# One stay of TensorE in its 64x64 tiles for each unit of a linear-attention and GELU-FFN kernel, with k transposed there by fp32 products

## The chip, the cores and the metric

The kernel runs on one core of a Trainium2 chip. The metric is the device time of one execution in microseconds (us): from the start of the program on the core to its end. Lower is better. Five engines are named by the profile: PE (TensorE, matrix products), with PEld for its weight loads, DVE (VectorE), ACT (ScalarE), POOL (GpSimd) and SP (SyncE, which issues most transfers here).

## The reference

Two stages follow each other. A gated linear attention keeps, for each of 4 batches and 8 heads, a 48x48 state that decays row by row with alpha and takes in the outer product of k and v at each of 768 positions; y is q times the state. The 3072 rows of y (8 heads x 48 = 384 columns) then go through a feed-forward net with 2048 hidden columns and an exact GELU.

```python
for t in range(S):                       # S = 768, D = 48
    state = alpha[:, :, t, :, None] * state + np.einsum('bhd,bhe->bhde', k[:, :, t], v[:, :, t])
    y[:, :, t] = np.einsum('bhd,bhde->bhe', q[:, :, t], state)
x = y.transpose(0, 2, 1, 3).reshape(B * S, H * D)     # 3072 x 384
h = x @ w_in                                          # 384 x 2048
g = 0.5 * h * (1.0 + erf(h / sqrt(2)))
out = g @ w_out                                       # 2048 x 384
```

## The kernel before

**Attention by units.** Positions are taken 256 at a time (12 groups, `g`), the heads in two halves (`u`), so there are 24 units, n = 2g + u. Names carry both numbers: `yc_3_0` belongs to g = 3, u = 0, which is unit 6. On DVE a unit's decays are run up as products (two scans forward, `pp`, two backward, `rp`), q is multiplied by the first and k by the second. On PE a unit has four steps, each of many small fp32 products that fill one of four 64x64 tiles of the array:

- `scores` (S, L351): k by q in four chunks of 64 positions, 16 products with 64 columns each. The profile shows an fp32 product as two rows, so 32 rows.
- `turned` (T, L359): k transposed, since the state needs it with positions along the partitions. Four 128x128 transposes against the identity, on the whole array.
- `inside` (I, L410 and L427): the masked scores by v, 16 products (32 rows), which begin y; then the turned k by v, 16 products with 48 columns (32 rows, 24 for the last group of a batch), which give the growth of the state by chunks.
- `outside_part` (O, L477): the states by q, which completes y: 16 products with 64 columns (32 rows), 12 (24 rows) for the first group of a batch.

Between S and I, DVE writes the masked scores (`ss`, L387) and ACT the turned k (`kn`, L381) to SBUF. Between I and O, DVE adds up the chunks' states (`chain`, L447). After O, y is split into a rounded float32r part and a remainder (`xh` on ACT, `xl` on DVE; for units 0 to 2 the remainder is made by a product with minus the identity on PE, `x_minus`, L562, and an ACT copy).

**Where a unit's results stand.** For the units 2 to 11, S and T of unit n write the same PSUM bank pair (`sbank` or `ybank`) in which I and O of unit n - 2 and of unit n itself build y. From unit 12 (`SPLIT`) on, S writes two other banks (`sh`, `sw`) and every y is built in `sbank`. So either S of unit n, or I of unit n - 1, can't start before y of unit n - 2 has been read. For units 4 to 9 that reading is one ACT copy of y to SBUF (`yc`, L557, `y_out`), and the split works from the copy; for the others the split itself reads the bank.

**The net.** Four blocks of 256 rows (`gemm1` L585, `gemm2` L677) and four of 512 rows (`wide1` L602, `wide2` L620) are multiplied in steps of 256 or 128 hidden columns. Each step is a first product, two GELU activations on ACT (`ghi` L654, rounded; `hp` or `hw` L658, in full), their difference on DVE (`glo`, L667) and a second product. x, the weights and the GELU's result are each split in two float32r parts, of which three products are taken. The weights are turned into such parts in 16 pieces during the first 85 us (ACT `top` L265 and L279, DVE L269 and L282, for pieces 1 to 3 with help of PE, L291).

**What sets the order.** A planner at build time places all steps on PE, DVE, ACT and SP by a table of costs (`COST`), by ranks (`ORDER`: digits are units, letters weight pieces) and by dependencies (`op(...)` in `plan_unit`). The order on each engine is then fixed; the hardware waits only for data. PE takes attention steps when they are ready, and steps of the net otherwise. `JOINED`, `SEAM`: from unit 6 on, the planner ties O, I and S of neighbouring units so that some of them follow each other directly.

Of the kernel before, what the change touches and what calls it, by code (L numbers as in the profile page):

```python
# [8 lines left out]
F32 = mybir.dt.float32  # L9
# [13 lines left out]
BY_PRODUCT = (1, 2, 3)  # L23
EARLY = 2
JOINED = 5
SEAM = 0.22
U_RANK, HI_RANK = 0.5, 0.4
X_BY_PRODUCT = (1, 2)
STEPS_BY_PRODUCT = 2
LOOK, EARLY_LOOK = 1.5, 1.0  # L30
RATE = 360.0
# [1 line left out]
WAIT = 0.2  # L33
SLOW = 1.0
COST = dict(
    turn=0.3, head=0.75, body=0.95, tail=0.49, sel=0.6, sel2=1.0, ends=0.22, differ=1.2, half=0.34, minus=0.4, gminus=0.35, rest=0.5, rest2=1.0,
    scan=0.65, scan2=0.65, back0=0.86, back=0.71, times=0.62, q=1.35, scores=1.24, kn=0.52, mask=0.62, mask1=0.4, kn1=0.36, inside=1.28, chain=1.1, outer=0.77, carry=0.22,
    xh=0.6, xl=0.72, spread=2.0, check=0.85, load=2.6, fetch=0.4, u=1.0, c0=0.56, c1=0.89, c2=0.56, c3=0.95, c4=0.92,
    hi=0.82, lo=0.89, gemm1=2.12, gelu=0.51, low=0.62, most=1.4, last=0.69, part=1.0,
    wide1=2.1, wide2=2.07, wpart=1.1,  # L40
)
ORDER = "0 1 a b c 2 d 3 e f 4 g h i j k 5 l m n o p"


@with_exitstack
def gla_then_gelu_ffn(ctx: ExitStack, tc: tile.TileContext, q, k, v, alpha, qg, kg, ag, vg, w_in, w_out, out):
    nc = tc.nc
    B, H, D, S = q.shape
    NF, P, NK, _ = w_in.shape
    DM, DFF = NK * P, NF * P  # L50
    NT = B * S
    C = 128
    G = 2 * C
    CS = C // 2
# [300 lines left out]
    def turned(g, u):  # L355
        d = cur[g, u]
        for j in range(NCH):
            e = (2 + j % 2) * C
            nc.tensor.transpose(  # L359
                out=d["s"][j // 2][:, e : e + C], in_=d["kt"][:, 2 * j * CS : 2 * (j + 1) * CS], identity=ident  # L360
            )

    def room(n):
        return stage if n % 2 and n < NU * NSB else work

    def kn_tile(g, u):
        d = cur[g, u]
        if "kn" not in d:
            d["kn"] = room(NU * g + u).tile([P, 2, 2 * P], F32, tag="kn", bufs=1, name=f"kn_{g}_{u}")
        return d["kn"]  # L370

    def ss_tile(g, u):
# [5 lines left out]
    def turned_out(g, u, bank=None):  # L378
        src = y_of(NU * g + u) if bank is None else cur[g, u]["s"][bank]
        to = kn_tile(g, u)  # L380
        nc.scalar.copy(to if bank is None else to[:, bank], src[..., 2 * C : 4 * C])  # L381

    def masked(g, u, bank=None):
        src = y_of(NU * g + u) if bank is None else cur[g, u]["s"][bank].unsqueeze(1)
# [9 lines left out]
    def inside(g, u):  # L394
        d = cur[g, u]
        ybank = y_of(NU * g + u)
        vn = vbuf[g % NB]
        spare = () if g else (0, 1)[: u + 1]
        for i in spare:
            nc.tensor.matmul(  # L400
                ybank[:, i, :G], lhsT=zeros, rhs=products[:, :G], start=True, stop=False, skip_group_check=True
            )
        for j in range(NCH):
            for i in range(2):
                r = slice(i * CS, (i + 1) * CS)
                for h in range(2):
                    rows = D if i in spare else DP
                    o = slice((h ^ i) * DP, (h ^ i) * DP + rows)
                    e = (2 * u + h) * D
                    nc.tensor.matmul(  # L410
                        ybank[o, i, j * CS : (j + 1) * CS],
                        lhsT=vn[r, j, e : e + rows],
                        rhs=d["ss"][r, h, j, :],
                        start=(j == 0 and i not in spare),
                        stop=(j == 0 and g % GPB == 0),
                        skip_group_check=True,
                    )
        for j in range(NCH):
            if ends_batch(g, j):
                continue  # L420
            t = 2 * C + j * D
            for i in range(2):
                r = slice(i * CS, (i + 1) * CS)
                for h in range(2):
                    o = slice(h * DP, (h + 1) * DP)
                    e = (2 * u + h) * D
                    nc.tensor.matmul(  # L427
                        ybank[o, i, t : t + D],
                        lhsT=d["kn"][r, j // 2, (j % 2) * P + h * DP : (j % 2) * P + (h + 1) * DP],
                        rhs=vn[r, j, e : e + D],  # L430
                        start=False,
                        stop=True,
                        skip_group_check=True,
                    )
# [400 lines left out]
    def op(*args, **kw):  # L835
        ops.append(Op(*args, **kw))
        return ops[-1]
# [4 lines left out]
    def plan_unit(n):  # L842
# [25 lines left out]
        d["back"] = op("DVE", "back", lambda: fns["b"](1), [half], rank=r)  # L868
        d["keys"] = op("DVE", "times", lambda: fns["k"](), [d["back"]], rank=r)
        shared = [pp_.get("out", pp_["xh"]), pp_.get("out", pp_["xl"])] if NU <= n <= SPLIT else []  # L870
        d["scores"] = op("PE", "scores", lambda: (scores(g, u), turned(g, u)), [d["keys"], d["q"], sp.get("mask"), sp.get("kn"), *shared], rank=r)
        if n >= SPLIT:
            d["scores"].deps.append(p["outer"])
            d["scores"].cost -= SEAM
            p["outer"].deps += [d["keys"], d["q"]]
        if JOINED < n <= SPLIT:
            pp_["outer"].deps += [p["mask"], p["kn"]]
            p["inside"].deps.append(pp_["outer"])
            p["inside"].cost -= SEAM
        if JOINED < n < SPLIT:  # L880
            pp_["outer"].deps += [d["keys"], d["q"]]
            d["scores"].deps.append(p["inside"])
            d["scores"].cost -= SEAM
        if n < NU or n >= SPLIT:
# [4 lines left out]
        else:  # L889
            d["mask"] = op("DVE", "mask", lambda: masked(g, u), [d["scores"], rp.get("inside")], rank=-1)  # L890
            d["kn"] = op("ACT", "kn", lambda: turned_out(g, u), [d["scores"], rp.get("inside"), d["mask"]], rank=-1)
        d["inside"] = op("PE", "inside", lambda: inside(g, u), [d["mask"], yp.get("xh"), yp.get("xl")], rank=r)
        if NU <= n < SPLIT:
            d["inside"].deps.append(d["kn"])
        else:
            d["inside"].soon = [d["kn"]]
        if n >= SPLIT:
            d["scores"].bank = d["mask"], d["kn"]
            if n > SPLIT:
                p["outer"].bank = ()  # L900
        d["chain"] = op("DVE", "chain", lambda: chain(g, u), [d["inside"], pp_.get("carry")], rank=-1 if n else 1.5)
        if n == 1:
            op("PE", "sel2", lambda: [selected(sbank[:, i, :G], i) for i in range(2)], [d["inside"], unit[0]["zh"]], rank=-1)
# [13 lines left out]
        if n == 0:  # L917
            d["zh"] = op("ACT", "half", z_out, [d["outer"]], rank=-1)
            d["sel"] = op("PE", "sel", lambda: selected(ybank[:, 0, :G], NK - 1), [d["zh"]], rank=-1)
            d["xh"] = op("ACT", "half", lambda: x_high(g, u), [d["sel"]], rank=-1)  # L920
            d["minus"] = op("PE", "minus", lambda: x_minus(g, u), [d["xh"]], rank=-1)
            d["xl"] = op("ACT", "half", lambda: x_rest(g, u), [d["minus"]], rank=-1)
        else:
            last_z = ready_x[g - 1] if u == 0 and g > 1 else []
            if JOINED <= n + 1 < SPLIT - 1:
                d["out"] = op("ACT", "kn", lambda: y_out(g, u), [d["outer"]], rank=-2)
            d["xh"] = op("ACT", "xh", lambda: (to_late(g, u), x_high(g, u)), [d["outer"], d.get("out"), *last_z], rank=-1)
        d["free"] = free if u == 0 else []
        if n == 0:
# [192 lines left out]
    def foreseen(o):  # L1122
# [5 lines left out]
                at = at and max(at, free_at["PE"]) + open_[0].cost + WAIT  # L1128
        return at

    def choose(e, t):
        best = None
        for o in waiting[e]:
            if o.cost == COST["differ"] and not steps:
                continue
            at = when(o)
            if at is not None and at <= t + 1e-9 and (best is None or (o.rank, o.n) < (best.rank, best.n)):
                best = o
        if e in ("DVE", "ACT") and best is not None and best.rank >= 0:
            urgent = [at for o in waiting[e] if o.rank < 0 for at in [foreseen(o)] if at is not None and at > t]  # L1140
            if urgent and t + best.cost - min(urgent) > (LOOK if steps else EARLY_LOOK) * (min(urgent) - t):
                return None
        if e != "PE":
            return best
        if best is not None:
            return best
        second = [s for s in steps if s["gemm2"].start is None]
        if second:
            o = second[0]["most"]
            if o is None or o.start is not None:  # L1150
                o = second[0]["gemm2"]
            at = when(o)
            if at is not None and at <= t + 1e-9:
                return o
        if len(second) < 2:
            free = bank_free()
            if free is not None and free <= t + 1e-9:
                g = next_step(t)
                if g is not None:
                    return gemm1_op(g, t)  # L1160
        if 8.0 < t and not steps:
            soon = [at for o in waiting["PE"] if o.cost != COST["differ"] for at in [when(o)] if at is not None]
            if (not soon or min(soon) > t + COST["turn"]):
                n = min(4, int((min(soon) - t - 0.06) / 0.24)) if soon else 1
                fill = Op("PE", "turn", lambda: turn_over(n))
                fill.cost = 0.06 + 0.24 * n
                return fill
        return None
# [127 lines left out]
```

## Time and profile before

| | |
|---|---|
| time, median of 3 runs | 502.43 us (502.13 to 504.56) |
| the profiled execution's own time | 502.19 us |
| its span, first to last instruction | 500.6 us |
| PE busy | 488.6 us, 98% of the span |
| DVE / ACT busy | 248.9 us / 195.4 us |
| granted TensorE clock | 0.996 of full speed |

The first 180 us hold the units 0 to 17 and the conversion of the weights beside the blocks of 256 rows; the units 18 to 23 stand at 274 to 303 and 352 to 371 us, between steps of the blocks of 512 rows. All else is the net alone.

### The profile page before, as it was taken

The numbers are of one execution on the slowest core, as the hardware profiler recorded it, in microseconds if no ns is written. First come the engines' busy times: TensorE is split into PE (matmuls) and PEld (weight loads), VectorE is DVE, ScalarE is ACT, GpSimd is POOL, SyncE is SP. The second block draws the span as 40 slices with busy tenths as digits, with TensorE's granted clock in tenths as the row PEclk, the third lists the DMA queues.
The fourth block names the chain that finished last, engine by engine and source line by source line (L and its number), as shares of the span: only waits on it lengthen the run. The fifth ranks groups of instructions, "written<-read, shape, count | busy, mean of one in ns | idle before, by whom it ended". The sixth has DMA issues, their size and how long they took to land.

```text
span 500.6 us, 12047 instructions
## 1 busy us (share of the span) xinstructions
PE 488.6 (98%) x5216; PEld 417.5 (83%) x5216; DVE 248.9 (50%) x485; ACT 195.4 (39%) x398; POOL 7.4 (1%) x21
## 2 busy tenths in 40 slices
PE   7999999999999999999999999999999999999994
PEld 5688999999999999988887878888778888888883
DVE  6988999998899971211112694212431212221212
ACT  4788766454534333213133442313241313231321
POOL 2000000000000000000000000000000000000000
PEclk9999999999999999999999999999999999999998
DMA  7996662554545410000000640000200000100001
GB/s 294 393 353 194 247 212 69 156 171 145 176 119 176 139 62 1 20 14 1 1 0 7 210 141 0 1 0 1 82 16 3 1 0 1 63 0 1 0 1 69
DMA packets 20845, 44.31 MB, mean 89 GB/s; under 512 B 2832, under 2 KB 4688, under 8 KB 20784
## 3 DMA queue, kind: packets, MB, share of 16 engines
q1 hardware_dynamic: 19136, 38.41, 23.4%
q0 software_dynamic: 880, 3.93, 2.1%
q10 hardware_dynamic: 768, 1.11, 0.6%
q8 instruction: 43, 0.70, 0.6%
q14 instruction: 18, 0.15, 0.1%
HBM read 36.57 MB, written 4.72 MB: 82 GB/s over the span
## 4 chain that ended last, share of the span: by engine, by line
PE 92%; DMA 4%; ACT 1%; DVE 1%; issue 0%; ACTq 0%; SPq 0%
PE hw L602 27%; PE accw L620 27%; PE acc L677 13%; PE hp L585 13%; DMA st<-in_moe_w_out_dram 2%; PE sbank L410 2%; PE sbank L477 2%; PE sbank L427 1%; DMA qd<-in_qg_dram 1%; PE sh L351 1%; PE sh L359 1%; PE sbank L359 1%; PE sbank L351 1%; PE ybank L477 1%; PE ybank L410 1%; PE sw L359 1%
## 5 line engine op out<-in xcount | busy, mean ns | idle before, releaser
L667 DVE TENSOR_TENSOR glo<-hw,ghi 128x512 fp32r<-128x512 f32 x64 | 44.3, 692 | 198.5 <-ACT hw L658 198.4
L602 PE MATMUL hw<-x,wih 128*128 128x512 f32 x384 | 121.2, 396 | 0.0
L654 ACT ACTIVATE ghi<-hw 128x512 fp32r<-128x512 f32 x64 | 38.3, 599 | 193.2 <-PE hw L602 193.2
L602 PEld LDWEIGHTS hw<-x,wih 128*128 128x128 f32 x384 | 71.5, 188 | 16.7
L620 PE MATMUL accw<-ghi,woh 128*128 128x512 f32 x192 | 76.2, 397 | 0.0
L602 PE MATMUL hw<-x,wil 128*128 128x512 f32 x192 | 75.8, 395 | 0.0
L620 PE MATMUL accw<-ghi,wol 128*128 128x512 f32 x192 | 75.2, 392 | 0.0
L585 PE MATMUL hp<-x,wih 128*128 128x256 f32 x384 | 70.0, 282 | 0.0
L585 PEld LDWEIGHTS hp<-x,wih 128*128 128x128 f32 x384 | 59.7, 188 | 0.5
L620 PE MATMUL accw<-glo,woh 128*128 128x512 f32 x192 | 55.7, 392 | 0.0
L585 PE MATMUL hp<-x,wil 128*128 128x256 f32 x192 | 53.7, 280 | 0.0
L677 PE MATMUL acc<-woh,ghi 128*128 128x384 f32 x128 | 44.5, 348 | 0.8 <-ACT ghi L654 0.8
L602 PEld LDWEIGHTS hw<-x,wil 128*128 128x128 f32 x192 | 36.0, 187 | 8.9
L677 PE MATMUL acc<-wol,ghi 128*128 128x384 f32 x128 | 43.1, 337 | 0.0
L620 PEld LDWEIGHTS accw<-ghi,woh 128*128 128x128 f32 x192 | 36.0, 188 | 8.2
L620 PEld LDWEIGHTS accw<-glo,woh 128*128 128x128 f32 x192 | 36.1, 188 | 7.9
L620 PEld LDWEIGHTS accw<-ghi,wol 128*128 128x128 f32 x192 | 36.1, 188 | 7.7
L658 ACT ACTIVATE hw<-hw 128x512 f32<-128x512 f32 x64 | 37.9, 593 | 0.0
L654 ACT ACTIVATE ghi<-hp 128x512 fp32r<-128x512 f32 x32 | 19.2, 600 | 47.0 <-PE hp L585 47.0
L585 PEld LDWEIGHTS hp<-x,wil 128*128 128x128 f32 x192 | 36.1, 188 | 0.1
L324 DVE TENSOR_TENSOR_SCAN rp<-ad,rp,bottom 128x255 f32<-128x255 f32 x48 | 34.1, 739 | 0.9
L311 DVE TENSOR_TENSOR_SCAN pp<-ad,bottom 128x256 f32<-128x256 f32 x48 | 31.3, 678 | 4.5 <-DMA ad<-in_ag_dram 4.4
(145 smaller groups left out, 577.5 us busy)
## 6 DMA issues: line engine op xcount, KB each, us to landing
st<-in_moe_w_in_dram SPq DMA_DIRECT2D x8, 768.0 KB, 7.3
st<-in_moe_w_out_dram SPq DMA_DIRECT2D x8, 768.0 KB, 7.6
qd<-in_qg_dram SPq DMA_DIRECT2D x23, 256.0 KB, 3.3
ad<-in_ag_dram SPq DMA_DIRECT2D x23, 256.0 KB, 3.6
kd<-in_kg_dram SPq DMA_DIRECT2D x23, 256.0 KB, 3.8
vn<-in_vg_dram SPq DMA_DIRECT2D x12, 416.0 KB, 5.2
out_dram<-parts POOLq DMA_DIRECT2D x3, 768.0 KB, 4.4
x<-z SPq DMA_DIRECT2D x60, 32.0 KB, 2.8
```

The costliest lines, as they stand in the source:

```text
L311: nc.vector.tensor_tensor_scan(pp[:, i], at[:, i], bottom, MID, ALU.mult, ALU.max)
L324: nc.vector.tensor_tensor_scan(rp[:, i, G - 2 :: -1], at[:, i, G - 1 : 0 : -1], bottom[:, 1:], rp[:, i, G - 1 :], ALU.mult, ALU.max)
L359: nc.tensor.transpose(out=d["s"][j // 2][:, e : e + C], in_=d["kt"][:, 2 * j * CS : 2 * (j + 1) * CS], identity=ident)
L410: nc.tensor.matmul(ybank[o, i, j * CS : (j + 1) * CS], lhsT=vn[r, j, e : e + rows], rhs=d["ss"][r, h, j, :], start=(j == 0 and i not in sp ...
L477: ins = nc.tensor.matmul(ybank[o, i, t], lhsT=states[u][j][r, i], rhs=d["qt"][r, i, t], start=False, stop=True, skip_group_check=True,)
L585: nc.tensor.matmul(hp[:, j, :], lhsT=a[:, j, i * P : (i + 1) * P], rhs=x[:, i, :], start=(start and m == 0), stop=(stop and (j, i, n) in t ...
L602: nc.tensor.matmul(h, lhsT=a[:, j, i * P : (i + 1) * P], rhs=x[:, i, part], start=(i == 0 and n == 0), stop=(i == NK - 1 and n == 2),)
L620: nc.tensor.matmul(acc[i], lhsT=w[:, j, e], rhs=a, start=(f == 0 and k == 0 and w is wo_hi[f2]), stop=(f == NF - 1 and k == 1),)
L654: nc.scalar.activation(ghi, hp, AF.Gelu)
L658: nc.scalar.activation(hp, hp, AF.Gelu)
L667: nc.vector.tensor_tensor(out=glo, in0=hp, in1=ghi.bitcast(F32), op=ALU.subtract)
L677: nc.tensor.matmul(acc[t], lhsT=a[:, j, t * C : (t + 1) * C], rhs=w[:, j, :], start=(first and j == 0 and k == 0 and w is wo_hi[f]), stop= ...
```

## The change

- **One visit.** From unit 6 on PE takes O of unit n - 2, I of unit n - 1 and S and T of unit n directly one after the other, without a step of the net between them: in the order O, I, S, T for units 6 to 12 and O, S, T, I from unit 13 on. Before, most of these units had two such stretches. Stretches of small products are 50 in the program before and 34 now; up to unit 5 there are 13 in both.
- **T by products.** k is transposed by 16 fp32 products with a 48-row piece of the identity, in the same 64x64 tiles as S and with the same weights, 48 columns each and 64 in the last chunk. `kn` gets 416 columns in place of 512.
- **The copy of y.** All units from 4 to 22 have it, with a rank ahead of the GELUs in the planner, and I waits for the copy, not for the split.
- **The planner** lets PE wait up to `HOLD` = 0.35 for the next step of a visit that has begun.
- **Early.** Unit 2 is ranked ahead of weight piece 2 (letter c): its loads are issued before that piece's, and its DVE steps stand before the piece's. Its remainder of x is made on DVE, not by PE products.

```diff
-SEAM = 0.22
+SEAM = 0.3
+HOLD = 0.35
-X_BY_PRODUCT = (1, 2)
+X_BY_PRODUCT = (1,)
-ORDER = "0 1 a b c 2 d 3 e f 4 g h i j k 5 l m n o p"
+ORDER = "0 1 a b 2 c d 3 e f 4 g h i j k 5 l m n o p"
...
     def turned(g, u):
         d = cur[g, u]
         for j in range(NCH):
-            e = (2 + j % 2) * C
-            nc.tensor.transpose(
-                out=d["s"][j // 2][:, e : e + C], in_=d["kt"][:, 2 * j * CS : 2 * (j + 1) * CS], identity=ident
-            )
+            n = D if j < NCH - 1 else DP
+            for i in range(2):
+                for h in range(2):
+                    r, e = slice(h * DP, h * DP + D), 2 * C + j * D
+                    nc.tensor.matmul(
+                        d["s"][h][i * CS : (i + 1) * CS, e : e + n],
+                        lhsT=d["kt"][r, (2 * j + i) * CS : (2 * j + i + 1) * CS],
+                        rhs=ident[r, h * DP : h * DP + n],
+                        start=True,
+                        stop=True,
+                    )
...
         d["scores"] = op("PE", "scores", lambda: (scores(g, u), turned(g, u)), [d["keys"], d["q"], sp.get("mask"), sp.get("kn"), *shared], rank=r)
-        if n >= SPLIT:
-            d["scores"].deps.append(p["outer"])
+        if n > SPLIT:
+            d["scores"].deps.append(pp_["outer"])
             d["scores"].cost -= SEAM
-            p["outer"].deps += [d["keys"], d["q"]]
+            pp_["outer"].deps += [d["keys"], d["q"], p["mask"], p["kn"]]
+            pp_["outer"].bank = ()
+            p["inside"].deps.append(d["scores"])
+            p["inside"].cost -= SEAM
...
-        if JOINED < n < SPLIT:
+        if JOINED < n <= SPLIT:
             pp_["outer"].deps += [d["keys"], d["q"]]
...
-        d["inside"] = op("PE", "inside", lambda: inside(g, u), [d["mask"], yp.get("xh"), yp.get("xl")], rank=r)
+        d["inside"] = op("PE", "inside", lambda: inside(g, u), [d["mask"], *of_y], rank=r)
...
-            if JOINED <= n + 1 < SPLIT - 1:
-                d["out"] = op("ACT", "kn", lambda: y_out(g, u), [d["outer"]], rank=-2)
+            if JOINED <= n + 1 < n_units:
+                d["out"] = op("ACT", "out", lambda: y_out(g, u), [d["outer"]], rank=-4)
...
+        if plan and steps:
+            before = max((o for o in plan[-40:] if o.eng == "PE"), key=lambda o: o.start, default=None)
+            for o in after.get(id(before), ()):
+                at = foreseen_all(o)
+                if o.start is None and at is not None and at <= t + HOLD:
+                    return None
```

On PE, at unit 7 (O of unit 5, I of unit 6, S and T of unit 7), the program before has:

```order
L477 MATMUL sbank_78<-qd0_102,state1_3_115 48x64 x4
L410 MATMUL ybank_79<-ss_3_0_1278,vn1_103 64x64 x16
L427 MATMUL ybank_79<-vn1_103,kn_3_0_1291 64x48 x16
L677 MATMUL acc0_1_0_966<-woh6_143,ghi_1343 128x384
L677 MATMUL acc0_1_0_966<-wol6_151,ghi_1343 128x384
```

and, four further rows of L677 later, still on PE before,

```order
L677 MATMUL acc1_1_0_967<-woh6_143,ghi_1343 128x384
L677 MATMUL acc1_1_0_967<-wol6_151,ghi_1343 128x384
L351 MATMUL sbank_78<-qd1_106,kd1_105 64x64 x16
L359 MATMUL sbank_78<-ident_73,kd1_105 128x128 x4
L677 MATMUL acc0_1_0_966<-woh6_143,glo_1347 128x384 x2
```

In the changed program the same place on PE reads:

```order
L485 MATMUL sbank_78<-qd0_102,state1_3_115 48x64 x4
L418 MATMUL ybank_79<-ss_3_0_1349,vn1_103 64x64 x16
L435 MATMUL ybank_79<-vn1_103,kn_3_0_1353 64x48 x16
L352 MATMUL sbank_78<-qd1_106,kd1_105 64x64 x16
L363 MATMUL sbank_78<-ident_73,kd1_105 64x48 x12
L363 MATMUL sbank_78<-ident_73,kd1_105 64x64 x4
L685 MATMUL acc0_0_3_1430<-woh4_141,ghi_1440 128x384
```

The eight rows of the net between I and S are gone, and the transposes have become 16 products.

On ACT, around the copy of y of unit 6 (`yc_3_0`), the program before has (`junk` is the range check of a unit's alpha, `ends` a two-column copy):

```order
L381 COPY kn_3_1_1466<-sbank_78 128x512
L213 ACTIVATE junk_9_1473,outside_97<-ad0_100,hi_b_93 128x512
L557 COPY yc_3_0_1523<-ybank_79 128x512
L314 COPY ends_98<-pp_4_1_1475 128x2
L549 CAST z3_1535<-yc_3_0_1523 128x256
```

and the changed program:

```order
L389 COPY kn_3_1_1557<-sbank_78 128x416
L583 DMA x2_1289<-z2_1290 16x512 x2
L214 ACTIVATE junk_9_1591,outside_97<-ad0_100,hi_b_93 128x512
L662 ACTIVATE ghi_1607<-hp_0_5_1570 128x512
L666 ACTIVATE hp_0_5_1570<-hp_0_5_1570 128x512
L565 COPY yc_3_0_1648<-ybank_79 128x512
```

Two GELUs now stand between the check and the copy: the first product of a step of the net precedes the visit directly on PE. It is so at five of the 18 visits, those that begin with O of the units 6, 7, 11, 13 and 19.

On ACT, ahead of the copy of y of unit 4 (`yc_2_0`), the program before has the casts of the last two weight pieces and then five steps that also stand before the copy:

```order
L265 CAST top1_159<-st_15_1095 128x768
L654 ACTIVATE ghi_1170<-hp_1_4_1126 128x512
L658 ACTIVATE hp_1_4_1126<-hp_1_4_1126 128x512
L279 CAST wih7_128<-st_14_1081 128x768
L654 ACTIVATE ghi_1194<-hp_1_5_1149 128x512
L658 ACTIVATE hp_1_5_1149<-hp_1_5_1149 128x512
L557 COPY yc_2_0_1228<-ybank_79 128x512
```

and the changed program:

```order
L666 ACTIVATE hp_1_5_1171<-hp_1_5_1171 128x512
L266 CAST top0_158<-st_14_1169 128x768
L266 CAST top1_159<-st_15_1197 128x768
L565 COPY yc_2_0_1284<-ybank_79 128x512
```

The copy now follows the cast of the last weight piece directly; S of unit 6 follows O of unit 4 in the same visit and waits for this copy.

## Rows read from the trace of the kernel before

**Rows 1.** The page, parts 1 and 4: busy us and shares; the chain by engine.

```profile
PE 488.6 (98%) x5216; PEld 417.5 (83%) x5216; DVE 248.9 (50%) x485; ACT 195.4 (39%) x398; POOL 7.4 (1%) x21
...
PE 92%; DMA 4%; ACT 1%; DVE 1%; issue 0%; ACTq 0%; SPq 0%
```

**Rows 2.** Windows: stretch, its length, busy us of each engine, clock, DMA share, GB/s.

```profile
40.00:50.00 10.00, 9.15 (x166) 8.08 (x165) 8.97 (x14) 8.71 (x18) 0.00 (x0) 1.00 0.69 209
...
60.00:80.00 20.00, 20.00 (x276) 19.18 (x275) 18.36 (x30) 14.23 (x24) 0.00 (x0) 1.00 0.58 196
```

**Rows 3.** Waits of PE: who waited for whom, us in total, times, longest.

```profile
PE acc L677 <- ACT ghi L654: 0.8, 1, 0.8
```

**Rows 4.** Timeline of PE at units 5 to 8: start, us, instruction, count.

```profile
87.08 0.40 PE L585 MATMUL hp<-x,wih 128*128 128x256 f32 x2
87.32 0.28 PE L585 MATMUL hp<-x,wil 128*128 128x256 f32 x1
87.53 0.67 PE L477 MATMUL sbank<-qd,state 48*48 48x64 f32 x32
88.01 0.65 PE L410 MATMUL ybank<-ss,vn 64*64 64x64 f32 x32
88.48 0.63 PE L427 MATMUL ybank<-vn,kn 64*64 64x48 f32 x32
89.04 0.44 PE L677 MATMUL acc<-woh,ghi 128*128 128x384 f32 x1
89.32 0.34 PE L677 MATMUL acc<-wol,ghi 128*128 128x384 f32 x1
89.50 0.34 PE L677 MATMUL acc<-woh,ghi 128*128 128x384 f32 x1
...
90.65 0.69 PE L351 MATMUL sbank<-qd,kd 48*64 48x64 f32 x32
91.27 0.66 PE L359 MATMUL sbank<-ident,kd 128*128 128x128 f32 x4
91.68 0.95 PE L677 MATMUL acc<-woh,glo 128*128 128x384 f32 x4
...
94.65 0.55 PE L477 MATMUL ybank<-qd,state 48*48 48x64 f32 x24
95.03 0.65 PE L410 MATMUL sbank<-ss,vn 64*64 64x64 f32 x32
95.49 0.63 PE L427 MATMUL sbank<-vn,kn 64*64 64x48 f32 x32
95.95 0.66 PE L351 MATMUL ybank<-qd,kd 48*64 48x64 f32 x32
96.54 0.66 PE L359 MATMUL ybank<-ident,kd 128*128 128x128 f32 x4
96.95 0.48 PE L585 MATMUL hp<-x,wih 128*128 128x256 f32 x2
```

**Rows 5.** Timeline of ACT at the same place, with idle time and releaser.

```profile
87.63 0.60 ACT L654 ACTIVATE ghi<-hp 128x512 fp32r<-128x512 f32 x1 [0.52 <-PE hp L585]
88.13 0.59 ACT L658 ACTIVATE hp<-hp 128x512 f32<-128x512 f32 x1
88.64 0.59 ACT L557 COPY yc<-sbank 128x512 f32<-128x512 f32 x1
...
95.27 0.59 ACT L557 COPY yc<-ybank 128x512 f32<-128x512 f32 x1 [1.28 <-PE ybank L477]
```

**Rows 6.** Timeline: the last piece's cast on ACT, and O of unit 4 on PE.

```profile
74.55 1.07 ACT L265 CAST top<-st 128x768 f16<-128x768 bf16 x1 [2.09 <-DMA st<-in_moe_w_out_dram]
...
76.27 0.67 PE L477 MATMUL ybank<-qd,state 48*48 48x64 f32 x32
```

**Rows 7.** Timeline of PE: the remainder of x of unit 2 by products, and what follows.

```profile
38.44 0.38 PE L562 MATMUL ybank<-z,minus 128*128 128x256 f32 x1
...
38.77 0.39 PE L182 MATMUL hp<-ghi,minus 128*128 128x512 f32 x1
```

More of the change, by code (lines that the diff above doesn't have):

```diff
@@ L36 @@
     turn=0.3, head=0.75, body=0.95, tail=0.49, sel=0.6, sel2=1.0, ends=0.22, differ=1.2, half=0.34, minus=0.4, gminus=0.35, rest=0.5, rest2=1.0,
-    scan=0.65, scan2=0.65, back0=0.86, back=0.71, times=0.62, q=1.35, scores=1.24, kn=0.52, mask=0.62, mask1=0.4, kn1=0.36, inside=1.28, chain=1.1, outer=0.77, carry=0.22,
+    scan=0.65, scan2=0.65, back0=0.86, back=0.71, times=0.62, q=1.35, scores=1.29, kn=0.44, out=0.52, mask=0.62, mask1=0.4, kn1=0.32, inside=1.28, chain=1.1, outer=0.77, carry=0.22,
     xh=0.6, xl=0.72, spread=2.0, check=0.85, load=2.6, fetch=0.4, u=1.0, c0=0.56, c1=0.89, c2=0.56, c3=0.95, c4=0.92,
@@ L368, in kn_tile @@
         if "kn" not in d:
-            d["kn"] = room(NU * g + u).tile([P, 2, 2 * P], F32, tag="kn", bufs=1, name=f"kn_{g}_{u}")
+            d["kn"] = room(NU * g + u).tile([P, 2, NCH * D + DR], F32, tag="kn", bufs=1, name=f"kn_{g}_{u}")
         return d["kn"]
@@ L380, in turned_out @@
         to = kn_tile(g, u)
-        nc.scalar.copy(to if bank is None else to[:, bank], src[..., 2 * C : 4 * C])
+        nc.scalar.copy(to if bank is None else to[:, bank], src[..., 2 * C : 2 * C + NCH * D + DR])
     def masked(g, u, bank=None):
@@ L428, in inside @@
                         ybank[o, i, t : t + D],
-                        lhsT=d["kn"][r, j // 2, (j % 2) * P + h * DP : (j % 2) * P + (h + 1) * DP],
+                        lhsT=d["kn"][r, h, j * D : j * D + DP],
                         rhs=vn[r, j, e : e + D],
@@ L870, in plan_unit @@
         shared = [pp_.get("out", pp_["xh"]), pp_.get("out", pp_["xl"])] if NU <= n <= SPLIT else []
+        of_y = [yp.get("out", yp.get(x)) for x in ("xh", "xl")]
         d["scores"] = op("PE", "scores", lambda: (scores(g, u), turned(g, u)), [d["keys"], d["q"], sp.get("mask"), sp.get("kn"), *shared], rank=r)
-        if n >= SPLIT:
-            d["scores"].deps.append(p["outer"])
+        if n > SPLIT:
+            d["scores"].deps.append(pp_["outer"])
             d["scores"].cost -= SEAM
-            p["outer"].deps += [d["keys"], d["q"]]
+            pp_["outer"].deps += [d["keys"], d["q"], p["mask"], p["kn"]]
+            pp_["outer"].bank = ()
+            p["inside"].deps.append(d["scores"])
+            p["inside"].cost -= SEAM
         if JOINED < n <= SPLIT:
@@ L879, in plan_unit @@
             p["inside"].cost -= SEAM
-        if JOINED < n < SPLIT:
+        if JOINED < n <= SPLIT:
             pp_["outer"].deps += [d["keys"], d["q"]]
+            if n == SPLIT:
+                pp_["outer"].bank = ()
             d["scores"].deps.append(p["inside"])
@@ L898, in plan_unit @@
             d["scores"].bank = d["mask"], d["kn"]
-            if n > SPLIT:
-                p["outer"].bank = ()
         d["chain"] = op("DVE", "chain", lambda: chain(g, u), [d["inside"], pp_.get("carry")], rank=-1 if n else 1.5)
@@ L1129, in foreseen, with foreseen_all @@
         return at
+    after = {}
+    for n in range(JOINED + 1, n_units):
+        chain_ = ("outer", n - 2), ("inside", n - 1), ("scores", n)
+        if n > SPLIT:
+            chain_ = chain_[0], chain_[2], chain_[1]
+        for (what, m), (then, to) in zip(chain_, chain_[1:]):
+            after[id(unit[m][what])] = (unit[to][then],)
+    def foreseen_all(o):
+        at = 0.0
+        for d in o.deps:
+            end = d.end
+            if end is None:
+                begin = when(d)
+                if d.eng != "ACT" or begin is None:
+                    return None
+                end = max(begin, free_at["ACT"]) + d.cost
+            at = max(at, end + (WAIT if d.eng != o.eng else 0.0))
+        return at
     def choose(e, t):
@@ L1146, in choose @@
             return best
+        if plan and steps:
[3 more added lines that the diff above has]
+                if o.start is None and at is not None and at <= t + HOLD:
+                    return None
         second = [s for s in steps if s["gemm2"].start is None]
```

## The prediction, made before the changed kernel ran

> **What bounds the kernel now.** I read the page first: PE is busy for 98% of the span and carries 92% of the chain that ended last [rows 1]. Then the windows: from 60 us on PE is busy all the time, with DVE close behind it at 18.36 of 20 us while the units are made; only before about 50 us does PE idle (9.15 of 10 us from 40 to 50) [rows 2], the longest such wait being 0.8 us for a GELU [rows 3]. So the end moves by what PE's work in sum gains, and by each new wait of PE: there is no slack on PE in which either could vanish. The price of a stretch of small products I read from the timeline of PE, start to start, since the durations of pipelined rows overlap [rows 4]. The timeline of ACT beside it shows when a copy of y can be done [rows 5].
>
> **What a stretch costs.** Steps of the net follow each other by 0.12 us (two rows from 87.08 to 87.32). O begins at 87.53, 0.09 later than the next step would have. I and its second half follow to 89.04, and the first product of the net behind them takes 0.28 in place of 0.18, so 0.10 more. This stretch costs 0.09 + 1.51 + 0.10 = 1.70 us. S and T of unit 7 stand alone from 90.65 to 91.68: with the same edges 0.09 + 1.03 + 0.10 = 1.22. Together 2.92 us [rows 4]. Unit 8 already has all in one stretch, 94.65 to 96.95: 0.09 + 2.30 + 0.10 = 2.49, with an O of 24 rows that takes 0.38, where one of 32 takes 0.48; with 32 it would be 2.59 [rows 4]. Joining thus gains 0.33 us. The order O, S, T, I has the same steps; I give it the same price.
>
> **T as products.** 32 rows of 64x64 tiles take 0.46 us, with 64 columns (95.03 to 95.49) and with 48 (95.49 to 95.95) [rows 4]. T is 32 such rows, so 0.46. Now S and T take 1.00 (95.95 to 96.95), of which 0.46 is S, 0.13 the passage to the whole array and 0.41 the transposes. Then: 0.46 + 0.46, and a passage of 0.10 at the end of the stretch, as the 48-column half of I pays in front of the net (0.56 at 88.48, 0.46 at 95.49) [rows 4]: 1.02 to 1.03. I take 0.03 more per unit. No row shows T's exact shape (48 rows of k by 48 columns). Bounds: 0.35, if columns alone counted (48 of 64), and 0.59, if the passage of 0.13 stayed. I take 0.46, since 48 and 64 columns cost the same in adjacent rows.
>
> The Trainium skill speaks against so many small products: "TensorE: Matmul & The Clock Gate", in its section on the warm-up ("Wait — 56ns, not 53.3ns?"), says that starts of products never come closer than about 25 ns however few the columns. That would make T 32 x 25 = 0.80 us, an estimate from that page. The trace disagrees for this tiling: 32 rows in 0.46 us are 14 ns each [rows 4].
>
> **Sum of PE's work.** 16 stretches fewer at 0.33, less 0.03 for their T: 16 x 0.30 = 4.8 us gained. The other eight T (units 0 to 5, 8, 9) cost 8 x 0.03 = 0.24. The products for unit 2's remainder go: 38.44 to 38.77, 0.33 gained [rows 7]. Gross: -4.8 + 0.24 - 0.33 = -4.9 us.
>
> **The waits that the joining adds.** S of unit n (I of unit n - 1 from unit 13 on) now comes right behind O of unit n - 2 and must wait for the copy of y. With ACT free, the copy starts 0.24 us after O's last start-to-start step (95.03 to 95.27) and takes 0.59; S began at 95.95, 0.09 after the copy's end and not late, so I count 0.05 from the copy to its user [rows 4, 5]. That is 0.88 us behind O, against 0.92 of other small products in between: no wait, just. Where I is of 28 products and not 32 (S of units 11 and 12), three quarters of a half are left, 0.46 + 0.35 = 0.81: 0.07 each, 0.14 in sum.
>
> Where a first product of the net stands directly ahead of O, its two GELUs are first in ACT's queue, and ACT takes its queue in order. The trace has that case at unit 5: O starts at 87.53, the GELUs at 87.63 and 88.13, the copy at 88.64, done at 89.23, 1.70 us after O's start [rows 4, 5]. Today nothing waits for it there. In the changed order it is so at O of units 6, 7, 13 and 19 (24 rows) and 11 (32 rows). The user could start after 0.38 + 0.92 = 1.30 or 0.48 + 0.92 = 1.40 us, and will at 1.75: 4 x 0.45 + 0.35 = 2.15 us lost. The rank ahead of the GELUs doesn't help, since the GELU's product ends before O even begins. Behind the waiting S or I stands the rest of PE's queue, so the loss is whole.
>
> At unit 4 the copy stands behind the cast of the last weight piece, 1.07 us long, which waited for its transfer; now it begins at 74.55 and is over 0.65 before O at 76.27 [rows 6]. In the new order S of unit 6 is in the same stretch. If the cast still ends before O, nothing is lost; if it starts as the copy could, 1.07, and more if the piece lands still later. I take 0.7, with 0 to 2.0 as bounds: the new order puts cast and copy next to each other, where today GELUs lie between.
>
> The extra copies on ACT hide under its idle time (39% busy [rows 1]). Waits in sum: 0.14 + 2.15 + 0.7 = 3.0 us.
>
> **The early stretch.** Unit 2's loads pass one weight piece on SP's queue and its scans pass that piece on DVE; the remainder of its x moves to DVE, which is busy for 8.97 of 10 us [rows 2]. The wait of 0.8 for a GELU [rows 3] can go, as PE's order changes there, or another can come, as a later piece holds back its steps of the net. I take 0, between -0.85, PE's idle time from 40 to 50 us [rows 2], and twice that lost.
>
> **Forecast.** -4.9 + 3.0 = -1.9 us on the profiled execution's 502.19: 500.3. That execution lies 0.24 under the median of 502.43, so 500.5 us. Its own range, with the early stretch and unit 6's wait at their bounds but not both at once: 499.0 to 502.2.
>
> **Rivals.** (1) *The early wait goes and the last cast is out of the way.* PE's order puts the GELU's product well ahead of its use, and the copy finds ACT free: -0.85 - 0.7, so 499.0. For it: ACT was idle before that cast. Against: DVE and ACT are nearly full early. (2) *T costs by its columns*, 0.35: 0.11 less for 21 units (in three of the five GELU cases T lies inside the wait): -2.3, so 498.2. Against: adjacent rows with 48 and 64 columns. (3) *Slower: the copy of y is late in every stretch.* The place is ACT's queue between O and S or I; the price 0.45 as behind two GELUs, now also at the other 12 stretches: 12 x 0.45 = 5.4, less the 0.14 counted: 505.8. It decides for slower from 0.37 us at each of the 12. For it: the margin there is 0.04. Against: no GELU stands between in the order, and the copy of unit 6 began 0.24 after O. (4) *The change doesn't do what it says: the array changes its shape for T anyway.* Then S to T costs 0.13 in all 24 units and T to I 0.10 in the 11 stretches that go on with I, less what the waits hide: 3.1 + 1.1 - 0.7 = 3.5, so 504.0. Against: in the rows O (48x48), I (64x64) and S (48x64) follow each other without it. (5) *The new products start 25 ns apart*, where S and I start 14 ns apart: 32 x 25 = 0.80, so T is 0.34 longer, at 21 units 7.1: 507.6. Against: the 14 ns of all the neighbours [rows 4]. The Trainium skill's page named above gives this spacing.
>
> **How the numbers follow.** Forecast 0.54, (1) 0.20, (2) 0.07, (3) 0.09, (4) 0.07, (5) 0.03. About 0.5% (2.5 us, 499.9 and 504.9) is what a measurement can tell from no change. Faster: (1), (2) and 0.13 of the forecast's own range below 499.9: 0.40. Slower: (3) and (5): 0.12. Within: 0.48. The range for 8 in 10 takes in the forecast, (1), half of (2) and a part of (4): 497.8 to 504.0.
>
> **What would show it.** The busy time of PE falls, and stretches of small products in PE's timeline number 34. Right for T: 32 rows in 0.44 to 0.48 us, and S to T without the 0.13. Right for the waits: ahead of S of units 6, 8 and 9 and I of units 12, 14 and 20, PE waits for ACT's copy `yc`, 0.35 to 0.45 at the five GELU cases, and the sum of these waits is near 3.0. PE stays busy all through 110 to 130 us. The prediction is wrong if those waits are under 1 us in sum, if T takes over 0.55, or if PE's idle time before 60 us changes by over 1.5 us.

## The result and the profile after

The changed kernel takes 509.5 us (median of 4 runs, 507.3 to 510.72) against 502.93 us before: a ratio of 1.0119 with a 95% interval of 1.0095 to 1.0143. It is slower; the forecast was 500.5, with 504.0 as its upper end. The profiled execution took 509.73 us, its span is 508.1, so 7.5 us more than before where 1.9 less were forecast: 9.4 us to find.

The page after (span and rows of each engine, the instruction queue, the chain by engine) answers to [rows 1]:

```profile
span 508.1 us, 13397 instructions
...
PE 489.5 (96%) x5888; PEld 420.2 (83%) x5888; DVE 252.2 (50%) x489; ACT 202.6 (40%) x409; POOL 7.4 (1%) x21
...
q8 instruction: 48, 0.79, 0.7%
...
PE 87%; DMA 4%; DVE 3%; ACT 2%; issue 2%; SPq 0%; ACTq 0%; DVEq 0%
```

PE has 672 rows more and as many weight loads, its share fell from 98 to 96%, and "issue" stands in the chain with 2% where it had 0. The waits of PE after (who waited for whom, us in total, times, longest) answer to [rows 3]:

```profile
PE ybank L485 <- issue: 3.2, 2, 2.2
PE sbank L435 <- issue: 2.0, 1, 2.0
...
PE ybank L352 <- ACT yc L565: 1.4, 2, 1.2
...
PE sbank L418 <- ACT yc L565: 0.7, 3, 0.3
PE sbank L352 <- ACT yc L565: 0.3, 1, 0.3
```

The waits for `yc` are the forecast ones. The first two rows are not: 5.2 us in which PE waits for no engine, no transfer and no semaphore that the profile shows. So it isn't so here that the hardware waits only for data, as the part on what sets the order has it. The timeline of PE shows them in the middle of a group of small products (start, us, instruction, count, idle time before):

```profile
13.75 0.32 PE L485 MATMUL ybank<-qd,state 48*48 48x64 f32 x5
16.23 0.54 PE L485 MATMUL ybank<-qd,state 48*48 48x64 f32 x19 [2.17 <-issue]
...
38.19 0.52 PE L485 MATMUL ybank<-qd,state 48*48 48x64 f32 x20
39.76 0.43 PE L485 MATMUL ybank<-qd,state 48*48 48x64 f32 x12 [1.05 <-issue]
...
285.38 0.63 PE L435 MATMUL sbank<-vn,kn 64*64 64x48 f32 x30
288.00 0.26 PE L435 MATMUL sbank<-vn,kn 64*64 64x48 f32 x2 [1.99 <-issue]
```

Five rows of O of unit 0 run, PE stands for 2.17 us, then the other 19 run. Nothing in the program separates them. Windows from the start to each stop give its place in PE's stream (stretch, length, busy us and rows of PE and PEld, and so on):

```profile
0.00:14.50 14.50, 11.92 (x222) 8.33 (x222) 10.57 (x22) 7.48 (x18) 2.67 (x14) 1.00 0.84 310
0.00:39.20 39.20, 32.31 (x603) 24.39 (x604) 28.53 (x56) 24.18 (x49) 2.67 (x14) 0.96 0.87 322
0.00:286.50 286.50, 276.41 (x4293) 248.85 (x4294) 186.92 (x362) 137.35 (x279) 6.29 (x19) 0.99 0.40 131
```

With the 5, 10 and 54 waiting instructions of PE's queue that the trace has up to there, these are 449, 1217 and 8641 instructions: 449 + 3 x 256 and 449 + 32 x 256. The queue named "instruction" moved 48 packets of 16 KB, 43 before; with 256 to a packet, the 11,859 and 10,507 instructions that the traces have of PE make 46.3 and 41.0. At the third stop, the view of transfers from 284.9 to 286.6 us has one such packet:

```profile
q8 instruction: 1, 0.02, 6.0%
```

It starts at 284.93, lasts 1.6 us, and PE goes on 3.1 us after its start. The theory from here on, FETCH: PE's instructions come in pages of 256 (a page from here on), and PE stops where it is through one page before the next is there. The profile doesn't say whose instructions a packet holds; this is inferred from places and counts, and from the times of all packets, told at the end.

The clock, windows as in [rows 2]:

```profile
15.00:20.00 5.00, 3.77 (x53) 3.12 (x57) 2.82 (x5) 2.54 (x7) 0.00 (x0) 0.74 1.04 395
20.00:25.00 5.00, 4.05 (x88) 3.42 (x81) 3.62 (x10) 2.92 (x6) 0.00 (x0) 0.92 1.04 393
```

After the first stop PE ran at 1.2 GHz from 17.4 to 20.8 us; the same stretch had 2.4 GHz before. The chain from `selected` to `x_minus` of unit 1 took 3.1 us there (17.95 to 21.06) in place of 2.2.

### The profile page after: what moved, and what is told of

Its sections match the earlier page's. It is cut to its first block, busy times and chain, and to the rows that moved or that the text cites. A ratio compares the mean times of both kernels' runs of the same rounds, so it can differ in the third digit from the quotient of the medians.

```text
span 508.1 us, 13397 instructions
## 1 busy us (share of the span) xinstructions
PE 489.5 (96%) x5888; PEld 420.2 (83%) x5888; DVE 252.2 (50%) x489; ACT 202.6 (40%) x409; POOL 7.4 (1%) x21
## 4 chain that ended last, share of the span: by engine, by line
PE 87%; DMA 4%; DVE 3%; ACT 2%; issue 2%; SPq 0%; ACTq 0%; DVEq 0%
PE accw L628 27%; PE hw L610 26%; PE hp L593 11%; PE acc L685 11%; PE sbank L418 2%; PE sbank L485 2%; DMA ad<-in_ag_dram 2%; PE sbank L435 1%; DMA st<-in_moe_w_in_dram 1%; DMA st<-in_moe_w_out_dram 1%; PE differ L292 1%; ACT yc L565 1%; PE ybank L352 1%; PE sh L352 1%; PE sh L363 1%
## 5 line engine op out<-in xcount | busy, mean ns | idle before, releaser
L610 PEld LDWEIGHTS hw<-x,wih 128*128 128x128 f32 x384 | 71.9, 188 | 17.4
```

What stands on the lines that cost most here:

```text
L610: nc.tensor.matmul(h, lhsT=a[:, j, i * P : (i + 1) * P], rhs=x[:, i, part], start=(i == 0 and n == 0), stop=(i == NK - 1 and n == 2),)
```

## What went as forecast

Unit 8's visit and ACT beside it, as [rows 4] and [rows 5]:

```profile
101.93 0.55 PE L485 MATMUL ybank<-qd,state 48*48 48x64 f32 x24
102.30 0.65 PE L418 MATMUL sbank<-ss,vn 64*64 64x64 f32 x32
102.77 0.63 PE L435 MATMUL sbank<-vn,kn 64*64 64x48 f32 x32
103.69 0.70 PE L352 MATMUL ybank<-qd,kd 48*64 48x64 f32 x32 [0.29 <-ACT yc L565]
104.20 0.65 PE L363 MATMUL ybank<-ident,kd 48*64 48x48 f32 x32
104.78 0.44 PE L685 MATMUL acc<-woh,ghi 128*128 128x384 f32 x1
```

```profile
102.03 0.60 ACT L662 ACTIVATE ghi<-hp 128x512 fp32r<-128x512 f32 x1 [0.32 <-PE hp L593]
102.53 0.59 ACT L666 ACTIVATE hp<-hp 128x512 f32<-128x512 f32 x1
103.04 0.59 ACT L565 COPY yc<-ybank 128x512 f32<-128x512 f32 x1
```

Two GELUs, then the copy, then S: 0.92 us from 102.77 to 103.69 where a half of I takes 0.46, so 0.46 lost, as forecast (0.45). The five cases lost 0.34 to 0.47. T's 32 rows take 0.47 with no 0.13 between S and T. At unit 6 the last weight piece's cast held back the copy:

```profile
81.55 0.52 PE L435 MATMUL sbank<-vn,kn 64*64 64x48 f32 x24
83.22 0.69 PE L352 MATMUL ybank<-qd,kd 48*64 48x64 f32 x32 [1.15 <-ACT yc L565]
```

```profile
81.67 1.05 ACT L266 CAST top<-st 128x768 f16<-128x768 bf16 x1 [2.38 <-DMA st<-in_moe_w_out_dram]
82.59 0.57 ACT L565 COPY yc<-ybank 128x512 f32<-128x512 f32 x1
```

24 rows of 0.35 took 1.67: 1.3 lost, within the bounds of 0 to 2.0, where 0.7 was taken.

## Experiments

**Shift the stream.** The first two put more PE instructions ahead of unit 0 and move nothing else:

```diff
-WARM = (1, 1, 4, 4, 2, 2)
+WARM = (1, 1, 4, 2, 2)
+EXTRA = 29
...
+    for m in range(EXTRA):
+        i, h = m // 2 % 2 * DP, m % 2 * DP
+        nc.tensor.matmul(
+            s_first[m % 2][i : i + DP, :DP], lhsT=ident[h : h + DP, :DP], rhs=ident[h : h + DP, :DP], start=True, stop=True
+        )
```

An fp32 product is four instructions (two rows, two loads), so 29 and one filling product less make 112; the second has `EXTRA = 48`, `WARM = (1, 1, 4, 2)`, 184.

> The changed kernel with 112 more PE instructions ahead of its first unit (29 small products on the identity, one filling product of four blocks replaced by one of two); nothing else moves. Theory FETCH: PE's instructions are brought in pages of 256 (the packets of 16 KB on the instruction queue, about 1 us each), and the three stops that the trace puts to 'issue' (O of unit 0 at 13.85 us, O of unit 2 at 38.7, I of unit 18 at 286; 5.2 us in sum) are where PE is through a page before the next one is there: all three stand at places 449, 1217 and 8641 of its stream, each 193 above a multiple of 256. A shift by 112 takes them away from all three places; one of about 1 us is left near 13 us (S of unit 1), and 0 to 0.9 us in sum behind 60 us (near 120 and 169 us). The sum of the stops on issue falls to 1 to 2 us, the clock stays at full rate after 8 us if the first is short, and the time is 504 to 506 us. Rival PLACE: the stops belong to these steps (their data, banks or the transfers beside them): they stay at O of unit 0, O of unit 2 and I of unit 18, and the time is 509 to 510.

Measured: 507.25 us, ratio 1.0089 [1.0069, 1.0109]. All three stops are gone from their places; the waits have

```profile
PE sfirst L360 <- issue: 1.1, 1, 1.1
...
PE sbank L443 <- issue: 0.7, 1, 0.7
```

the first at S of unit 1 at 13.1 us, place 449 again; the other, not foreseen, at 19.7, one page later. Behind 60 us none is left. The time fell by 2.2 us only, not to the 504 to 506 expected, and the intervals of the two ratios overlap; in the profiled execution these two stops were followed by two times of 1.2 GHz (15.9 to 19.3 and 22.7 to 26.2 us).

> The same with 184 more PE instructions (48 small products, two filling products fewer). Theory FETCH: page ends now fall at the end of the visits of small products at seven other places, near 96, 113, 129, 147, 177, 194 and 314 us, 0.2 to 1.6 us each, 4 to 8 us in sum, beside 1 to 2 us in the first 40 us; nothing at O of unit 2 or I of unit 18. Time 510 to 515. Rival PLACE: stops where they were, time 509 to 510.

Measured: 510.46 us, ratio 1.0153 [1.0133, 1.0173]. Five of the seven places show a stop, at 93.7, 111.6, 127.8, 176.9 and 314.3 us, 4.3 us in sum. Two of them, and the windows to them:

```profile
93.70 0.45 PE L693 MATMUL acc<-woh,ghi 128*128 128x384 f32 x1
95.15 0.34 PE L693 MATMUL acc<-wol,ghi 128*128 128x384 f32 x1 [1.01 <-issue]
...
314.00 0.52 PE L443 MATMUL sbank<-vn,kn 64*64 64x48 f32 x24
315.73 0.33 PE L443 MATMUL sbank<-vn,kn 64*64 64x48 f32 x8 [1.21 <-issue]
```

```profile
0.00:94.50 94.50, 87.95 (x1623) 78.40 (x1624) 81.65 (x147) 64.91 (x119) 2.67 (x14) 1.00 0.69 237
...
0.00:315.00 315.00, 303.92 (x4930) 271.43 (x4930) 210.52 (x415) 150.08 (x310) 6.29 (x19) 1.00 0.41 131
```

With 18 and 61 waiting instructions: 3265 = 449 + 11 x 256 and 9921 = 449 + 37 x 256. Where a stop falls follows the count of instructions and not the step; PLACE is refuted.

**The tile's width.** In the net after, nine second products of the 512-row blocks take 2.10 us (421.59 to 423.69), before 2.07 (423.04 to 425.11); 18 in a row take 4.190 and 4.132 us, medians of 24. No line of them was changed. The first rows of the nine and of what follows them, before and after:

```profile
423.04 0.40 PE L620 MATMUL accw<-ghi,woh 128*128 128x512 f32 x1
...
425.11 0.63 PE L602 MATMUL hw<-x,wih 128*128 128x512 f32 x2
```

```profile
421.59 0.39 PE L628 MATMUL accw<-ghi,woh 128*128 128x512 f32 x1
...
423.69 0.39 PE L628 MATMUL accw<-ghi,woh 128*128 128x512 f32 x1
```

```diff
-            d["kn"] = room(NU * g + u).tile([P, 2, NCH * D + DR], F32, tag="kn", bufs=1, name=f"kn_{g}_{u}")
+            d["kn"] = room(NU * g + u).tile([P, 2, 2 * P], F32, tag="kn", bufs=1, name=f"kn_{g}_{u}")
...
-        nc.scalar.copy(to if bank is None else to[:, bank], src[..., 2 * C : 2 * C + NCH * D + DR])
+        e = NCH * D + DR
+        nc.scalar.copy(to[..., :e] if bank is None else to[:, bank, :e], src[..., 2 * C : 2 * C + e])
```

> The changed kernel with the tile for the turned k 512 columns wide as before, of which 416 are written; no instruction is added or moved. Theory ADDRESS: the second products of the 512-row blocks (18 rows in 4.190 us in the changed kernel, 4.132 before, 32 steps of 36 rows) slow down because the narrower tile moves the tiles behind it in SBUF: they go back to 4.13 and the time falls by 1.7 us to 507 to 508. Rival: the spacing is a matter of the instructions or of the chip's state; it stays at 4.19 and the time at 509 to 510. The three stops on issue stay either way.

Measured: 509.41 us (506.82 to 511.43), ratio 1.0119 [1.0077, 1.0161]. The 18 products are back at 4.132, and are so in each of the nine kernels run with 512 columns, at 4.190 in the three with 416: 32 x 0.058 = 1.9 us. The time doesn't show it: it stayed where the rival had it. This profiled execution had a second time at 1.2 GHz, after the stop at 285.7, among 512-column products, some 1.6 us dearer:

```profile
289.00:293.00 4.00, 4.00 (x12) 3.10 (x12) 3.93 (x9) 1.04 (x3) 0.00 (x0) 0.57 0.51 180
```

The clocks of the other executions point the same way: the four have 0.989, 0.993, 0.989 and 0.992, the changed kernel's four 0.994, 0.998, 0.991 and 0.993. That is 0.003 less in the mean, at most 1.6 us over the span (an estimate; low clock behind PE's last row counts in it), about what the width gave back. That the width is the cause of the spacing is shown, its worth in time is reckoned from the spacing; how the width changes the spacing is open.

**Transposes in the joined visits**: `turned`, `turned_out` and `kn` as in the kernel before, the rest as changed.

```diff
-            n = D if j < NCH - 1 else DP
-            for i in range(2):
...
+            e = (2 + j % 2) * C
+            nc.tensor.transpose(
+                out=d["s"][j // 2][:, e : e + C], in_=d["kt"][:, 2 * j * CS : 2 * (j + 1) * CS], identity=ident
+            )
```

> The changed kernel with k turned by the four transposes of before and its tile of 512 columns; same order on all engines, visits joined. A visit then has 264 PE instructions or fewer in place of 320. Theory FETCH: no stop on issue over 0.2 us behind 30 us, at most 0.6 us ahead of that; the joining's gain of some 5 us stands against 3 to 3.5 us of waits for the copy of y: 500 to 502.5 us. Rival JOINING: the loss comes with the joined visits themselves, whatever T is: 506 to 510.

Measured: 504.22 us, ratio 1.0033 [1.0019, 1.0047]; 5.3 us better than the change by the medians, 4.3 by the ratios, and not one wait on "issue". JOINING is refuted; the time is still above the 502.5 expected. The profiled execution, which took 507.03 us, shows a wait at unit 6 that has a part in this: S began at 80.36, 2.3 us late, and 1.2 GHz stood from 80.1 to 83.5:

```profile
77.52 0.52 PE L428 MATMUL sbank<-vn,kn 64*64 64x48 f32 x24
80.36 1.13 PE L352 MATMUL ybank<-qd,kd 48*64 48x64 f32 x32 [2.33 <-ACT yc L558]
```

**One part alone, in the kernel before.** First `turned`, `turned_out` and `inside` as changed (the lines of the diff above, the other way), with 512 columns; then the early part:

```diff
-X_BY_PRODUCT = (1, 2)
+X_BY_PRODUCT = (1,)
-ORDER = "0 1 a b c 2 d 3 e f 4 g h i j k 5 l m n o p"
+ORDER = "0 1 a b 2 c d 3 e f 4 g h i j k 5 l m n o p"
```

> The kernel before with only one part of the change: k turned by the 16 products (tile of k 512 columns wide, so that no address moves); order and visits as before. Theory FETCH with the prediction's price of T: T by products costs 0.03 us a unit, 0.7 in sum; visits are shorter than the 256 instructions of a page between net steps (S and T 128, O and I 192, 320 only at units 8 and 9), so no stop on issue behind 60 us; two stops ahead of 42 us, where the transfers fill all queues and a page takes about 6 us: at O of unit 0 (near 14 us, place 449) and O of unit 2 (place 1217), 2 to 3.5 us in sum, the first followed by a time of half clock. Time 504.5 to 507. Rival: T's products are dearer than their rows say wherever they stand (0.2 us a unit or more), 508 or above; or the stops need the joined visits, and the time is 503.5.

Measured: 508.72 us, ratio 1.0117 [1.0099, 1.0134]: alone, T by products loses almost what the whole change loses. The time is above FETCH's 504.5 to 507 and in the range of the rival (508 or above), but not for the rival's reason: S and T together are 0.8 us dearer in all 24 units (24.8 to 25.6, forecast 0.72), where it asked 0.2 a unit.

```profile
PE ybank L485 <- issue: 2.2, 1, 2.2
```

That is the one stop, at O of unit 0 (place 449), with 1.2 GHz from 17.8 to 21.2 behind it; the second, at unit 2, came to 0.1 us only. Behind 60 us one of 0.1 is all. Not foreseen was a wait that wasn't there before: 1.1 us of an I for the remainder of x at 293 us.

> The kernel before with only the early part of the change: unit 2 ahead of weight piece 2, its remainder of x on DVE. The prediction took 0 for it, between -0.85 and +1.7. Theory EARLY: by the changed kernel's trace it costs 1 to 2 us by itself (a wait of 0.9 for a state and of 1.1 in place of 0.8 for a weight piece, less the 0.33 of products that go): 503.5 to 505. Rival: it gains or costs nothing, 502.5 to 503.3, and all early losses of the changed kernel are stops of the fetch, the clock behind them and the wait of unit 6.

Measured: 502.85 us, ratio 0.9998 [0.9985, 1.0011]: the rival holds, the early part by itself costs nothing.

**Towards a better version.** These two lines as before in the joined kernel with transposes; then, on top, in the planner's `choose`:

```diff
+        if e == "ACT" and best is not None and best.name == "gelu":
+            copies = [at for o in waiting[e] if o.name == "out" for at in [foreseen(o)] if at is not None]
+            if any(t < at <= t + 1.2 for at in copies):
+                return None
```

> The joined visits with the four transposes (504.2 us) and the early part as before. The wait of 2.3 us ahead of S of unit 6, behind the last weight piece's cast, goes, since the planner then puts casts and copy apart; so does the half clock that followed it in the slower executions. Theory: joining by itself is a gain: 500 to 502 us. Rival: the waits for the copies of y and the passages between the array's shapes eat the gain: 503 to 504.5.

> The same, and the planner holds ACT back from the two GELUs when a copy of y is foreseen within 1.2 us, so that GELUs stand behind the copy where they stood ahead of it. PE's waits for copies of y fall under 0.4 us in sum (about 1 us before): 0.3 to 1 us below the kernel without this, 499.5 to 501.5, if no step of the net then waits for its GELU; if one does, it is slower by that wait.

Measured: 502.62 us, ratio 0.999 [0.9976, 1.0003], 1.6 us less, with unit 6's wait down to 0.4, but 0.6 above the expected end; then 501.07 us, ratio 0.9959 [0.9939, 0.9979]. All waits of PE in the latter, and ACT at unit 7:

```profile
PE sfirst L136 <- POOL ident masks.py:199: 1.7, 1, 1.7
PE sbank L464 <- DVE state L448: 1.0, 1, 1.0
PE differ L292 <- ACT wil L297: 0.9, 1, 0.9
PE sbank L411 <- issue: 0.7, 1, 0.7
PE sfirst L352 <- DVE kd L331: 0.2, 1, 0.2
```

```profile
88.12 0.58 ACT L558 COPY yc<-sbank 128x512 f32<-128x512 f32 x1 [1.65 <-PE sbank L478]
88.60 0.60 ACT L655 ACTIVATE ghi<-hp 128x512 fp32r<-128x512 f32 x1
```

No wait for a copy of y is left. This version beats both kernels. The last three put T's products, and the shift, into it:

> The 501.1 us kernel (joined visits, early part as before, GELUs behind the copy of y) with T as the 16 products in place of the four transposes and nothing else (the tile of k keeps its 512 columns). Theory FETCH: T's rows by themselves gain about 1 us here, since the 11 visits of the order O, S, T, I no longer leave the 64x64 tiles; against that stand stops on issue at page ends: 2 to 2.5 us at O of unit 0 near 14 us with half clock behind it (1 to 2 us), 1 to 1.3 at O of unit 2 near 38 us, and near 139, 187 and 285 us 0.5 to 2 us each (near 89 and 156 us up to 0.9), 2 to 4.5 in sum; the stop of 0.7 at I of unit 1 goes. Time 505 to 508.5. Rival: the losses of the changed kernel hung on its early order or on the GELUs ahead of the copies; without these the products are as good as the transposes, 500 to 502.

Measured: 503.54 us, ratio 1.0016 [1.0003, 1.0029], 2.5 us worse than with transposes; stops at 14.2, 38.4, 139.5, 156.7, 187.2 and 283.9 us, all at 449 plus multiples of 256 and at six of the seven places named:

```profile
PE ybank L486 <- issue: 2.6, 2, 2.1
...
PE sbank L436 <- issue: 1.5, 2, 1.2
...
PE acc L686 <- issue: 0.5, 1, 0.5
```

They sum to 4.6 us where 5 to 8 was expected, and S and T gain 2.5 us (26.9 to 24.4), more than the 1 expected. The profiled execution took 505.45 us, with 1.2 GHz from 17.8 to 24.7; a smaller loss and a larger gain than expected go with the median below 505.

> The same with 200 more PE instructions ahead of the first unit (52 small products, two filling products fewer), a shift at which page ends fall mostly between visits or into their first half. Theory FETCH: no stop over 0.5 us ahead of 60 us; behind it stops near 94 and 112 us of 0.2 to 1.4 each, 0.8 to 2.3 in sum. Time 501 to 503.5, so 3 us or more below the same program unshifted. Rival: shift changes nothing, time as the unshifted program's.

Measured: 503.13 us, ratio 0.9998 [0.998, 1.0017]. Behind 60 us one stop of 0.5, at 93 us. But two early ones, 1.6 at 11.0 us (place 449) and 0.7 at 18.2, were not foreseen. The time is in the range named, but the gain on the unshifted program is 0.4 us, not 3: while the first transfers fill the queues, no shift tried was free of a stop with the denser stream.

> The 501.1 us kernel (with transposes) with 160 more PE instructions ahead of the first unit (41 small products, one filling product of four blocks replaced). Its only stop on issue, 0.7 us at I of unit 1 near 16 us (place 449), goes, since the page then ends at S of unit 1, ahead of which PE has waited for DVE; no other appears. Theory FETCH: 0 to 0.9 us gained, 500.2 to 501.1, at most; what follows the stop in that stretch (waits for a state and for a weight piece) may take it back. Rival: 501 to 502, no gain.

Measured: 500.92 us, ratio 0.9958 [0.9943, 0.9972]. No wait on "issue" is left; the 0.7 went into a wait of unit 1's I for the masked scores (0.9). No gain that can be told from none.

## Why the prediction was wrong

- **What bounds the kernel**: right; PE does, and every loss found is a wait or a slower row of PE.
- **What a stretch costs, T as products**: right. 34 stretches; T's 32 rows take 0.47 us, 14.6 ns each. Of the rule of "TensorE: Matmul & The Clock Gate" in the Trainium skill (section "Wait — 56ns, not 53.3ns?"), starts no closer than about 25 ns, the trace shows the contrary in these 64x64 tiles; rival (5) gave 507.6 for a reason that wasn't there.
- **The step that failed** is "Sum of PE's work": it counted PE's work in time alone. It priced 672 more rows, so 1344 more instructions, by their rows and never asked what brings them. A joined visit is 152 or 160 rows, 304 or 320 instructions in some 2.4 us; in the wide blocks a page of 256 lasts 128 rows of 0.23, 29 us. Before, the longest visit had 124 rows, 248 instructions, and ended with slower transposes. Cost in the profiled execution: 5.2 us of stops and about 1 us of half clock behind the first.
- The Trainium skill describes the pages ("Runtime: NRT & Kernel Launch", section "Instruction fetch mechanics": blocks of 16 KiB, 256 instructions, fetched by the sequencer's own queue) and calls the cost of a block's end mostly hidden. The trace agrees on the size (0.79 MB in 48 packets). On the hiding it agrees at 42 of the 45 page ends from place 449 on; at the other three PE stood for 2.2, 1.1 and 2.0 us. The prediction had not weighed this page.
- **T's tile**: "`kn` gets 416 columns" stood in the change and had no term; it cost 1.7 us (1.9, less 0.2 that the first products of these blocks gained, 4.195 to 4.190 us for 18).
- **Waits of the joining**: the mechanism and the five GELU cases were right. Unit 6 was mis-sized, 1.3 us for 0.7.
- **The early stretch**: the chosen 0 holds for that part alone (502.85 us). In the changed kernel PE's idle time up to 60 us still rose from 5.3 to 7.4 us, which the prediction had named as a sign that it is wrong: the stops of units 0 and 2 are in it.
- **The sum**: 5.2 + 1.0 + 1.7 + 0.6 (waits of the joining) + 0.1 for T (0.8 for 0.72, taken from the run with T's products alone) = 8.6 of the 9.4 us. The rest, 0.8, is not assigned.
- **Busy time of PE** was to fall and rose by 0.9. Against the joining's gain stand the slower second products (1.7), the half clock (about 1) and the filling products ahead of unit 0, which ran for 5.99 us in place of 5.01, where before PE then waited for `kd`. That is 3.7 against a forecast gain of 4.9; what else is in the 0.9 is not worked out.

So the idea was half right. Joining with the transposes, the early part as before and the copy ahead of the GELUs gives 501.07 us, 0.4% below the kernel before; T by products, the part that runs through pages faster than they come, takes it back (503.54).

## What to carry to other kernels

Count instructions, not only time: where a long run of short products passes several hundred instructions in two or three microseconds, the next page may not be there, and a wait on "issue" in the middle of a uniform group, at places that differ by multiples of 256 in the engine's stream, is its mark. Shifting the stream by harmless instructions tells this from causes that belong to the step, its data or its banks. After making a tile narrower, compare the spacing of rows that were not touched.

## What the runs showed of the hardware

- When a page is there: the third stop's packet started at 284.93 us, 0.9 us ahead of the page's end (285.8), and PE went on 3.1 us after that start; at the first stop, with the DMA share at 1.04, the packet started at 13.80, at the page's end, and PE went on 2.4 us after. Take, in each of the 13 traces, the packets in order, the first for what follows place 449, each next for what follows 256 places later. Of 557 page ends, 29 came less than 2.1 us after the start of their packet, and PE stopped at all 29; 525 came more than 2.18 us after, and it stopped at none; of the three between it stopped at two. It went on 2.3 to 3.1 us after the start, 1.2 to 1.5 us after the end of the packet.
- A short page alone isn't enough: in the changed kernel pages of 1.84 and 1.86 us ended at 176.3 and 158.3 without a stop, as their packets had started 3.0 and 2.9 us ahead. The page that ended at 285.8 had lasted 1.91. What sets the start of a packet is not shown.
- After seven of the eight stands of PE of 1.6 us or more (the one at its first instruction left out), its clock fell to 1.2 GHz, for 3.4 us, once for 6.8: at 17.4 us in the changed kernel, at 289.0 with the wide tile, at 80.1 in the joined kernel with transposes about its 2.3 us wait for `yc`. In the changed kernel's profile the stop of 2.0 at 286 was followed by none. Runs of the changed kernel spread by 3.4 us (507.3 to 510.7) as their clock did (0.998 to 0.991). What decides isn't shown.
- Second products with 512 columns take 229, 232 and 226 ns in turn with one layout of SBUF and 231 and 236 with another.
